# A two-layer network behind a light convolution, one core: TensorE reads the two halves of its moving tile in turns, and ScalarE and GpSimd take over work of VectorE and ScalarE

## The chip, the cores and the metric

The kernel runs on one core of a Trainium2 chip. The metric is the device time in microseconds (us) of one execution. The kernel before took 2235.05 us, the median of three runs (2235.0 to 2235.06).

The core has four engines that compute and run side by side, each taking its own instructions strictly in their order: TensorE (PE in the profile; its weight loads are listed apart as PEld), VectorE (DVE), ScalarE (ACT) and GpSimd (POOL). SyncE (SP) issues the DMAs. TensorE writes into PSUM, an on-chip memory of eight banks of 512 fp32 values per partition; VectorE and ScalarE read it from there. Everything else lies in SBUF.

## The reference

```python
# x: (8, 4096, 192), weight: (8 heads, 7 taps), w_in: (192, 2048), w_out: (2048, 192), all fp32
w = softmax(weight, axis=-1)
out[b, s, h, :] = sum over k of w[h, k] * x_padded[b, s + k, h, :]    # 7 taps, causal, 24 channels a head
x = out.reshape(32768, 192)
h = x @ w_in
g = np.where(h >= 1, h, np.where(h <= -1, 0.0, (h + 1) ** 2 / 4))
return g @ w_out
```

## The kernel before, in words

The 32768 tokens are cut into 64 tiles of 512 (`s`, 0 to 63), and the 2048 hidden features into 8 pairs of 128-feature blocks (`j`, 0 to 7). One step `q = 8 s + j` makes the hidden features of one pair for one tile; there are 512 steps. Two tiles, 16 steps, make a round (`i = q % 16`), and the convolution of a later pair of tiles is spread over the steps of a round.

TensorE does two things in a step. `mm1(q)` (L411) is the first product: 9 pairs of matmuls, each pair being two matmuls of 64 rows that run side by side in the two halves of the array, with 512 moving columns; they fill `h`, two PSUM banks, of which there are two sets (`ps_h`, bufs=2). `mm2(q - 2)` (L451) is the second product of the step two before: 10 such pairs, which add into four PSUM banks `accm0`, `accm1`, `accr0`, `accr1`; these exist once, so the second product of the next tile has to wait until ScalarE has copied them out. From the second round on all operands are split into a high part (fp32r) and a low remainder, `hi`/`lo` of x, `gh`/`gl` of g and two parts of each weight. The first 16 steps (`q < NF32`) work otherwise, in plain fp32 with the roles of the operands swapped in the second product, and are not touched.

Between the two products stands the activation, which the other engines do in each step, in this order of their queues:

- ScalarE: `act_hi(q-1)` (L480, g to gh), `act_square(q)` (L468).
- VectorE: `act_clip(q)` (L462, clips h to -1..1 out of PSUM), `act_lo(q-1)` (L486, gl = g - gh, both inputs in SBUF), `act_max(q)` (L473, max of h and the square). Only `act_max` sets the banks of h free.

Further work hangs on certain steps of a round. In steps 1 and 9 ScalarE copies the four `acc` banks of the tile that was just finished (`evac`, L497 and L498) behind its square, and GpSimd adds them (`sum`, L500). In steps 2 and 10 come a copy and an add of the rest (L510, L511), and in steps 2, 3, 10, 11 VectorE transposes the sums (L523) for the stores. The convolution has three units in a round, called `b`, `a` and `r`, with 7 taps each: a transpose on VectorE (`T`, L147), the product of tap 0 on ScalarE (L226), six products on ScalarE (`product`, L219), six adds on GpSimd (L230), and then the split: a copy on ScalarE (L248, L262) and a subtraction on GpSimd (L252) or VectorE (L263). Which tap falls into which step is a table:

```python
    PLAN_B = {0: (0, 1), 2: (2, 3), 3: (4, 5), 4: (6,), 5: "split"}
    PLAN_A = {4: ("T", 0), 5: (1, 2), 6: (3, 4), 7: (5, 6), 8: "split"}
    PLAN_R = {7: ("T",), 8: (0, 1, 2), 10: (3, 4), 11: (5, 6), 13: "split"}
```

In a step these taps stand behind `act_max` and `act_square`; unit `b` is transposed at the end of step 15. The order of each engine's queue is the order in which the program is written. The functions `both_square` (relu of h/2 + 1/2, then its square, both on ScalarE) and `most` (min with 1, max with h, on VectorE) exist already and are used in the first steps (L742, L744, L749).

Of the kernel before, what the change touches and what calls it, by code (L numbers as in the profile page):

```python
# [13 lines left out]
AF = mybir.ActivationFunctionType  # L14
ALU = mybir.AluOpType
# [3 lines left out]
P = 128  # L19
TB = 512  # L20
# [10 lines left out]
def lightconv_then_ffn(ctx: ExitStack, tc: tile.TileContext, x, weight, w_in, w_out, out):  # L31
# [24 lines left out]
    nc = tc.nc  # L56
    B, S, D = x.shape
# [7 lines left out]
    NPAIR = NF // 2  # L65
    DR = D - P
    NG = TB // SQ + 1
    TOP, BOT = slice(0, DR), slice(DR, P)
    HALVES = (TOP, BOT)
# [14 lines left out]
    def load_raw(t0s, chans, engs=None, n=TB):  # L84


        raw = xin.tile([P, NG, SQ], F32, name="raw")
        first = [t0 % S == 0 for t0 in t0s]
        for i0 in (0, 2):
            if first[i0]:  # L90
                nc.gpsimd.memset(raw[i0 * SQ:(i0 + 2) * SQ, 0, :], 0.0)
        for i in range(4):
            lo = 1 if first[i] else 0
            src = xf[t0s[i] - SQ + lo * SQ:t0s[i] + n, chans[i]:chans[i] + SQ]
            (engs[i] if engs else nc.sync).dma_start(
                out=raw[i * SQ:(i + 1) * SQ, lo:n // SQ + 1, :],
                in_=src.rearrange("(j a) b -> a j b", a=SQ),
            )
        return raw
# [10 lines left out]
    def load_unit(c, u, engs=None):  # L110
# [5 lines left out]
            return load_raw([ta, ta, tb, tb], [P, P + SQ, P, P + SQ], engs)  # L116
        return load_raw([ta if u == "a" else tb] * 4, [0, SQ, 2 * SQ, 3 * SQ], engs)

    xop = [dict() for _ in range(NSB)]

    pending = []
# [10 lines left out]
    NF32 = 2 * NPAIR  # L132
    SH = NG * SQ - TB - (K - 1)

    class Conv:
# [80 lines left out]

        def product(self, k):
            p = xw.tile([P, TB], F32, name="p", bufs=3)
            nc.scalar.mul(p, self.xT[:, SH + k:SH + k + TB], wk[:, self.wsel, k:k + 1])  # L219
            return p  # L220

# [77 lines left out]
    wk = const.tile([P, 2, K], F32, name="wk")  # L299
    warm = const.tile([P, 1], F32, name="warm")  # L300
    whose = const.tile([P, 2 * P + 72], F32, name="whose")[:, 0:2 * P]
    ident = const.tile([P, P], F32, name="ident")
# [87 lines left out]
    NQ = NSB * NPAIR  # L390
    hs, g32, gs, ghs, gls, accs = {}, {}, {}, {}, {}, {}

    def mm1(q):

        s, j = divmod(q, NPAIR)

        if q == 0:
            h = hs[q] = [ps_o.tile([P, TB], F32, name=n) for n in ("accr1", "accm0")]
        else:
            h = hs[q] = ps_h.tile([P, 2, TB], F32, name="h")  # L400
            h = [h[:, e, :] for e in range(2)]

        if s == 0:
            mms = [(WI[j], us, [xop[s][u] for u in us]) for us in ("ns", "sn", "rr")]
        else:
            mms = [(W[j][:, part], u + u, [xop[s][u, x]] * 2) for u in "nsr"
                   for part, x in ((0, "hi"), (1, "hi"), (0, "lo"))]
        for n, (w, us, x) in enumerate(mms):
            for e in range(2):
                c0 = COL[us[e]][e]  # L410
                nc.tensor.matmul(h[e], w[HALVES[e], c0:c0 + P], x[e][e],  # L411
                                 start=(n == 0), stop=(n == len(mms) - 1))

    def new_accs(s):
        accs[s] = {(a, i): ps_o.tile([P, TB], F32, name=f"acc{a}{i}")
                   for a in "mr" for i in range(2)}
# [16 lines left out]
    def mm2(q):  # L433

        s, j = divmod(q, NPAIR)
        gh, gl = ghs.pop(q), gls.pop(q)
        w, wr, k = W[j + LAG], WR[j + LAG], n_in[j + LAG]
        if j == 0:
            new_accs(s)
        m0, m1, r0, r1, r = ("m", 0, gh), ("m", 1, gh), ("m", 0, gl), ("r", 0, gh), ("r", 0, gl)  # L440
        mms = [(e, m) for ms in ((m0, m1), (r0,), (r1,), (r,)) for e in range(2) for m in ms]
        if q == NQ - 1:
            mms = [(0, m) for m in (r1, m0, m1, r, r0)] + [(1, m) for m in (r1, r, m0, m1, r0)]
        first = {a: min(n for n, (e, m) in enumerate(mms) if m[0] == a) for a in "mr"}
        last = {a: max(n for n, (e, m) in enumerate(mms) if m[0] == a) for a in "mr"}
        for n, (e, (a, part, g)) in enumerate(mms):
            c0 = k + e * P
            for i in range(2):
                st = (w[HALVES[i], part, c0:c0 + P] if a == "m"
                      else wr[HALVES[i], e].rearrange("p a d -> p (a d)"))  # L450
                nc.tensor.matmul(accs[s][a, i], st, g[HALVES[i], e, :],  # L451
                                 start=(j == 0 and n == first[a]),
                                 stop=(j == NPAIR - 1 and n == last[a]))


    def tiles(q):
        return [slice(0, 1), slice(1, 2)] if q == NQ - 1 else [slice(0, 2)]

    def act_clip(q):
        g = gs[q] = act.tile([P, 2, TB], F32, name="g", bufs=3)  # L460
        for e in tiles(q):
            nc.vector.tensor_scalar(out=g[:, e, :], in0=hs[q][:, e, :], scalar1=-1.0, scalar2=1.0,  # L462
                                    op0=ALU.max, op1=ALU.min)

    def act_square(q):
        g = gs[q]
        for e in tiles(q):
            nc.scalar.activation(g[:, e, :], g[:, e, :], AF.Square, bias=0.5, scale=0.5)  # L468

    def act_max(q):  # L470
        h, g = hs.pop(q), gs[q]
        for e in tiles(q):
            nc.vector.tensor_tensor(out=g[:, e, :], in0=h[:, e, :], in1=g[:, e, :], op=ALU.max)  # L473
        if q < NF32:
            g32[q] = gs.pop(q)
# [14 lines left out]
    def evac(s):  # L490

        acc = accs.pop(s)
        n = slice(0, 2 * D if s * NPAIR < NF32 else TB)
        for a in "mr":
            t = [ob.tile([P, TB], F32, name="t", bufs=4) for _ in range(2)]
            y = ob.tile([P, TB], F32, name="sum")
            nc.scalar.copy(t[0][:, n], acc[a, 0][:, n])  # L497
            nc.scalar.copy(t[1][:, n], acc[a, 1][:, n])  # L498
            if s > 0:
                nc.gpsimd.tensor_add(y[:, n], t[0][:, n], t[1][:, n])  # L500
            else:
                late.append((y[:, n], t[0][:, n], t[1][:, n]))
            sums[s, a] = y
# [32 lines left out]
    def evac_last(s):  # L536


        acc = accs.pop(s)
        half, rest = slice(0, TB // 2), slice(TB // 2, TB)  # L540
        part = {}
        for a in "rm":
            u, v = [ob.tile([P, TB], F32, name="t", bufs=4) for _ in range(2)]
            for n in (half, rest):
                nc.scalar.copy(u[:, n], acc[a, 0][:, n])
                nc.vector.tensor_tensor(out=v[:, n], in0=acc[a, 1][:, n], in1=u[:, n], op=ALU.add)
            part[a] = v
        ps = [ps_h.tile([P, 2, TB], F32, name="h")[:, 0] for _ in range(2)]
        ps += [ps_o.tile([P, TB], F32, name=f"accr{i}") for i in range(2)]
        y = [ob.tile([P, TB], F32, name="sum") for _ in range(2)]  # L550
        for b in range(TB // P):
            nc.tensor.matmul(ps[b][:, P:D], part["r"][:, b * P:(b + 1) * P], ident[:, 0:DR],  # L552
                             start=True, stop=True)
        for i in range(2):
            for b in (2 * i, 2 * i + 1):
                nc.tensor.transpose(ps[b][:, 0:P], part["m"][:, b * P:(b + 1) * P], plain)
            for b, copy in ((2 * i, nc.scalar.copy), (2 * i + 1, nc.vector.tensor_copy)):
                copy(y[i][:, b % 2 * D:(b % 2 + 1) * D], ps[b][:, 0:D])
                if i == 1:
                    (nc.sync if b % 2 else nc.scalar).dma_start(  # L560
                        out=out[s * TB + b * P:s * TB + (b + 1) * P],
                        in_=y[i][:, b % 2 * D:(b % 2 + 1) * D])
            if i == 0:
                nc.sync.dma_start(
                    out=out[s * TB:s * TB + 2 * P].rearrange("(b p) d -> p b d", p=P),
                    in_=y[i][:, 0:2 * D].rearrange("p (b d) -> p b d", b=2))
# [180 lines left out]
    def most(h, g):  # L747

        nc.vector.scalar_tensor_tensor(out=g, in0=g, scalar=1.0, in1=h, op0=ALU.min, op1=ALU.max)  # L749
# [75 lines left out]
    for q in range(NQ + DELAY):  # L825
        s, j = divmod(q, NPAIR)
        c, i = divmod(q, 2 * NPAIR)
# [11 lines left out]
        if q < NQ:  # L839
            mm1(q)  # L840
# [7 lines left out]
        else:  # L848
# [6 lines left out]
            if q < NQ:  # L855
                let_go()
                act_clip(q)
                act_square(q)
            if done % NPAIR == NPAIR - 1 and done >= NPAIR:
                (evac if done < NQ - 1 else evac_last)(done // NPAIR)  # L860
# [10 lines left out]
            m, r = (DELAY, DELAY + 1) if s > 1 else (NPAIR - 2, NPAIR - 1)  # L871
# [7 lines left out]
        if q == NQ - 4:  # L879
            plain = ob.tile([P, TB // SQ, SQ], F32, name="osb").rearrange("p j b -> p (j b)")[:, 0:P]  # L880
# [27 lines left out]
```

## Time and profile before

| | |
|---|---|
| median of the runs | 2235.05 us (2235.0 to 2235.06) |
| profiled execution, first to last instruction | 2233.2 us |
| PE busy | 2227.3 us (100%) |
| PEld busy | 1850.7 us (83%) |
| DVE busy | 2093.3 us (94%) |
| ACT busy | 1693.7 us (76%) |
| POOL busy | 1173.8 us (53%) |
| DMA | 110.84 MB, mean 50 GB/s |

The page is of one execution under the profiler. Its span leaves out what lies before the first and behind the last instruction; against the median of the timed runs that is 1.85 us, so that a change of the span can be read as a change of the time. Busy time counts only that an engine holds an instruction: matmuls overlap, and a PE busy all the time need not be one at its highest rate.

### The profile page before, as it was taken

Reading aid. Unit: us, or ns where it says so; the run is one execution under the profiler, and the core shown is the slowest. Engines: PE = TensorE matmul, PEld = TensorE weight load, DVE = VectorE, ACT = ScalarE, POOL = GpSimd, SP = SyncE. Lnnn points to the kernel's source line nnn. Section 1 sums busy time; section 2 is a strip of 40 time slices with the busy share of each in tenths; the row PEclk is TensorE's granted clock in tenths of the full one; section 3 lists DMA queues with packets and bytes.
Section 4 is the critical chain, followed back from the end, with each engine's and each line's share of the span. In section 5 each row is a group of like instructions: output and inputs, shape, how many; then the busy total and the mean of one; then the engine's idle time right before and its main releaser. Section 6 shows DMA issues by size and latency. Waiting matters only on the chain.

```text
span 2233.2 us, 48204 instructions
## 1 busy us (share of the span) xinstructions
PE 2227.3 (100%) x19646; PEld 1850.7 (83%) x19646; DVE 2093.3 (94%) x1883; ACT 1693.7 (76%) x2153; POOL 1173.8 (53%) x868
## 2 busy tenths in 40 slices
PE   9999999999999999999999999999999999999999
PEld 6988888888888888888888888888888888888887
DVE  8899999999999999999999999999999999999998
ACT  7677877778777787777877777877778777787775
POOL 1456644556545565455664456644556545565451
PEclk9999999999999999999999999999999999999999
DMA  6222222221222212222122222222221222212211
GB/s 160 49 52 48 42 47 47 52 53 39 52 49 46 54 34 52 49 49 51 40 47 48 49 51 50 41 49 46 50 54 39 52 49 46 54 34 52 49 34 25
DMA packets 442125, 110.84 MB, mean 50 GB/s; under 512 B 410288, under 2 KB 417840, under 8 KB 441904
## 3 DMA queue, kind: packets, MB, share of 16 engines
q1 hardware_dynamic: 441744, 107.66, 24.5%
q8 instruction: 155, 2.54, 0.5%
q14 instruction: 66, 0.54, 0.1%
q10 hardware_dynamic: 160, 0.10, 0.0%
HBM read 32.84 MB, written 25.17 MB: 26 GB/s over the span
## 4 chain that ended last, share of the span: by engine, by line
PE 99%; ACT 0%; DMA 0%; DVE 0%; issue 0%; DVEq 0%; ACTq 0%
PE h L411 47%; PE accm L451 30%; PE accr L451 20%; PE accr L429 1%; PE accm L429 1%; PE accr L190 0%; PE accr L411 0%; DMA osb<-in_weight_dram 0%; PE accm L181 0%; PE h L552 0%; ACT xT L168 0%; ACT xT L165 0%; ACT xT L167 0%; PE accm L411 0%; PE h L155 0%
## 5 line engine op out<-in xcount | busy, mean ns | idle before, releaser
L230 POOL TENSOR_TENSOR y<-y,p 128x512 f32<-128x512 f32 x546 | 798.2, 1462 | 733.3 <-DVE g L473 560.7
L411 PE MATMUL h<-hi,w 64*128 64x512 f32 x4032 | 764.7, 387 | 0.0
L486 DVE TENSOR_TENSOR gl<-g,gh 128x1024 fp32r<-128x1024 f32 (+1 forms) x497 | 730.4, 1470 | 29.3 <-ACT gh L480 24.2
L468 ACT ACTIVATE g<-g 128x1024 f32<-128x1024 f32 (+1 forms) x505 | 535.5, 1061 | 234.8 <-DVE g L462 228.5
L480 ACT CAST gh<-g 128x1024 fp32r<-128x1024 f32 (+1 forms) x497 | 522.8, 1052 | 226.8 <-DVE g L473 185.2
L462 DVE TENSOR_SCALAR g<-h 128x1024 f32<-128x1024 f32 (+1 forms) x505 | 609.1, 1206 | 85.5 <-PE h L411 84.4
L451 PE MATMUL accm<-gh,w 64*128 64x512 f32 x3968 | 639.6, 387 | 0.0
L473 DVE TENSOR_TENSOR g<-h,g 128x1024 f32<-128x1024 f32 (+1 forms) x505 | 613.3, 1215 | 11.8 <-ACT g L468 4.5
L411 PEld LDWEIGHTS h<-hi,w 64*128 64x128 f32 x4032 | 561.3, 185 | 75.4
L411 PE MATMUL h<-lo,w 64*128 64x512 f32 x2016 | 613.0, 387 | 0.0
L451 PEld LDWEIGHTS accm<-gh,w 64*128 64x128 f32 x3968 | 463.6, 184 | 75.6
L451 PE MATMUL accr<-gh,wr 64*128 64x512 f32 x1984 | 414.8, 387 | 0.0
L451 PE MATMUL accr<-gl,wr 64*128 64x512 f32 x1984 | 414.8, 386 | 0.0
L451 PE MATMUL accm<-gl,w 64*128 64x512 f32 x1984 | 414.7, 387 | 0.0
L411 PEld LDWEIGHTS h<-lo,w 64*128 64x128 f32 x2016 | 371.3, 184 | 38.1 <-DMA lo<-lo 0.2
L219 ACT ACTIVATE p<-xT,wk 128x512 f32<-128x512 f32 x562 | 374.9, 709 | 0.0
L451 PEld LDWEIGHTS accm<-gl,w 64*128 64x128 f32 x1984 | 276.4, 184 | 37.9
L451 PEld LDWEIGHTS accr<-gh,wr 64*128 64x128 f32 x1984 | 276.3, 184 | 37.8
L451 PEld LDWEIGHTS accr<-gl,wr 64*128 64x128 f32 x1984 | 276.2, 184 | 37.9
L411 PE MATMUL h<-rhi,w 64*128 64x512 f32 x992 | 304.1, 386 | 0.0
L411 PE MATMUL h<-rh,w 64*128 64x512 f32 x992 | 304.1, 386 | 0.0
L500 POOL TENSOR_TENSOR sum<-t 128x512 f32<-128x512 f32 (+1 forms) x124 | 157.4, 1291 | 101.8 <-ACT t L498 101.8
(143 smaller groups left out, 1945.4 us busy)
## 6 DMA issues: line engine op xcount, KB each, us to landing
out_dram<-osb SPq DMA_DIRECT2D x366, 64.0 KB, 1.9
raw<-in_x_dram SPq DMA_DIRECT2D x334, 68.0 KB, 2.4
hi<-hi SPq DMA_DIRECT2D x126, 128.0 KB, 2.3
lo<-lo SPq DMA_DIRECT2D x126, 128.0 KB, 2.3
rhi<-rh SPq DMA_DIRECT2D x62, 128.0 KB, 2.2
rlo<-rl SPq DMA_DIRECT2D x62, 128.0 KB, 2.3
words<-in_moe_w_in_dram SPq DMA_DIRECT2D x16, 192.0 KB, 3.6
words<-in_moe_w_out_dram SPq DMA_DIRECT2D x8, 384.0 KB, 4.8
```

What stands on the lines that cost most here:

```text
L219: nc.scalar.mul(p, self.xT[:, SH + k:SH + k + TB], wk[:, self.wsel, k:k + 1])
L230: nc.gpsimd.tensor_add(y, y, self.product(k))
L411: nc.tensor.matmul(h[e], w[HALVES[e], c0:c0 + P], x[e][e], start=(n == 0), stop=(n == len(mms) - 1))
L429: nc.tensor.matmul(accs[s][a, i][:, c0:c0 + D], g[half, e, b * P:(b + 1) * P], w[half, e, :], start=(j == 0 and e == 0 and b % 2 == 0), st ...
L451: nc.tensor.matmul(accs[s][a, i], st, g[HALVES[i], e, :], start=(j == 0 and n == first[a]), stop=(j == NPAIR - 1 and n == last[a]))
L462: nc.vector.tensor_scalar(out=g[:, e, :], in0=hs[q][:, e, :], scalar1=-1.0, scalar2=1.0, op0=ALU.max, op1=ALU.min)
L468: nc.scalar.activation(g[:, e, :], g[:, e, :], AF.Square, bias=0.5, scale=0.5)
L473: nc.vector.tensor_tensor(out=g[:, e, :], in0=h[:, e, :], in1=g[:, e, :], op=ALU.max)
L480: nc.scalar.copy(gh[:, e, :], gs[q][:, e, :])
L486: eng.tensor_sub(gl[:, e, :], g[:, e, :], gh[:, e, :])
L500: nc.gpsimd.tensor_add(y[:, n], t[0][:, n], t[1][:, n])
```

## The change

The moving operand of a matmul was read column by column, 0 to 511. Now `turns` makes TensorE read column 0, 256, 1, 257 and so on: the halves of the tile in turns. The result is written to consecutive columns of PSUM, so the tokens come out in another order. In the first product this holds from tile 2 on (`in_turns`), in the second always. Passing two products, the tokens are permuted twice, and `evac` undoes it: its ScalarE copies read PSUM in order and write SBUF in steps of 128 elements. The last tile is put in order by the products that transpose it, which read every fourth column.

In 8 of the 16 steps of a round (`BY_ACT`) the clip of VectorE is left out; ScalarE makes a relu out of PSUM and a square of it instead, two instructions where it had one, and VectorE's maximum becomes the three-input `most`. Six of the 21 tap products of a round (`BY_POOL`) move from ScalarE to GpSimd. This begins with step 16 and the third pair of tiles.

```diff
+    BY_POOL = (('b', 4), ('b', 5), ('a', 5), ('a', 6), ('r', 5), ('r', 6))
...
         def product(self, k):
             p = xw.tile([P, TB], F32, name="p", bufs=3)
+            if self.c > 1 and (self.u, k) in BY_POOL:
+                nc.gpsimd.tensor_scalar(out=p, in0=self.xT[:, SH + k:SH + k + TB],
+                                        scalar1=wk[:, self.wsel, k:k + 1], scalar2=None,
+                                        op0=ALU.mult)
+                return p
             nc.scalar.mul(p, self.xT[:, SH + k:SH + k + TB], wk[:, self.wsel, k:k + 1])
...
+    def turns(t):
+        return t.rearrange("p (o c) -> p c o", o=2)
+    def both(t):
+        return t.rearrange("p (c o) -> p c o", o=2)
+    def in_turns(s):
+        return s * NPAIR >= NF32
...
-                nc.tensor.matmul(h[e], w[HALVES[e], c0:c0 + P], x[e][e],
+                to, of = (both(h[e]), turns(x[e][e])) if in_turns(s) else (h[e], x[e][e])
+                nc.tensor.matmul(to, w[HALVES[e], c0:c0 + P], of,
...
-                nc.tensor.matmul(accs[s][a, i], st, g[HALVES[i], e, :],
+                nc.tensor.matmul(both(accs[s][a, i]), st, turns(g[HALVES[i], e, :]),
...
+    BY_ACT = (3, 4, 7, 11, 12, 13, 14, 15)
+    def by_act(q):
+        return q % (2 * NPAIR) in BY_ACT and NF32 <= q < NQ - 2
     def act_clip(q):
         g = gs[q] = act.tile([P, 2, TB], F32, name="g", bufs=3)
+        if by_act(q):
+            nc.scalar.activation(g, hs[q], AF.Relu, bias=0.5, scale=0.5)
+            return
...
     def act_square(q):
         g = gs[q]
+        if by_act(q):
+            nc.scalar.activation(g, g, AF.Square)
+            return
...
-        for e in tiles(q):
+        if by_act(q):
+            most(h, g)
+        for e in () if by_act(q) else tiles(q):
             nc.vector.tensor_tensor(out=g[:, e, :], in0=h[:, e, :], in1=g[:, e, :], op=ALU.max)
...
-            nc.scalar.copy(t[0][:, n], acc[a, 0][:, n])
-            nc.scalar.copy(t[1][:, n], acc[a, 1][:, n])
+            for i in range(2):
+                to, of = t[i][:, n], acc[a, i][:, n]
+                if in_turns(s):
+                    to = to.rearrange("p (b o a) -> p a b o", b=2, o=2)
+                    of = of.rearrange("p (a b o) -> p a b o", b=2, o=2)
+                nc.scalar.copy(to, of)
...
-            nc.tensor.matmul(ps[b][:, P:D], part["r"][:, b * P:(b + 1) * P], ident[:, 0:DR],
+            nc.tensor.matmul(ps[b][:, P:D], part["r"][:, b::TB // P], ident[:, 0:DR],
...
-                nc.tensor.transpose(ps[b][:, 0:P], part["m"][:, b * P:(b + 1) * P], plain)
+                nc.tensor.transpose(ps[b][:, 0:P], part["m"][:, b::TB // P], plain)
```

Three places show what this does to the queues. In the listings a row is one instruction (xN: N alike in a row): line, operation, out<-in and size. The lines of the changed kernel are its own: L485 is the relu, L494 its square, L497 the square of the other steps, L511 gh, L254 the copy hi, L232 and L225 tap products, L533 the copies out of the accumulators; on GpSimd L221 is a product, L236 an add, L258 the subtraction of the split; on VectorE L488 is the clip, L517 gl, L504 and L784 the maximum in its two forms, L148 the transpose.

ScalarE before, from the end of step 7 into step 9 of a round:

```order
L219 ACTIVATE p<-xT,wk 128x512 x2
L480 CAST gh<-g 128x1024
L468 ACTIVATE g<-g 128x1024
L248 CAST hi_15422<-y 128x512
L226 ACTIVATE y<-xT,wk 128x512
L219 ACTIVATE p<-xT,wk 128x512 x2
L480 CAST gh<-g 128x1024
L468 ACTIVATE g<-g 128x1024
L497 COPY t<-accm_15045 128x512
```

ScalarE in the changed kernel, from step 7 into step 9:

```order
L485 ACTIVATE g<-h 128x1024
L494 ACTIVATE g<-g 128x1024
L511 CAST gh<-g 128x1024
L497 ACTIVATE g<-g 128x1024
L254 CAST hi_15422<-y 128x512
L232 ACTIVATE y<-xT,wk 128x512
L225 ACTIVATE p<-xT,wk 128x512 x2
L511 CAST gh<-g 128x1024
L497 ACTIVATE g<-g 128x1024
L533 COPY t<-accm_15045 128x128x4
```

The two products of step 7 are gone from ScalarE and a relu stands ahead of its square; the four tap and split instructions of step 8 still stand ahead of gh of step 8, of the square of step 9 and of the copies out of the accumulators.

GpSimd before, from the adds that end unit b (steps 3 and 4) to the first adds of unit r in step 8:

```order
L230 TENSOR_TENSOR y<-y,p 128x512 x3
L252 TENSOR_TENSOR lo_11564<-y,hi_11563 128x512
L230 TENSOR_TENSOR y<-y,p 128x512 x6
L252 TENSOR_TENSOR lo_11736<-y,hi_11735 128x512
L230 TENSOR_TENSOR y<-y,p 128x512 x2
```

GpSimd in the changed kernel, the same stretch:

```order
L236 TENSOR_TENSOR y<-y,p 128x512 x2
L258 TENSOR_TENSOR lo_15251<-y,hi_15250 128x512
L236 TENSOR_TENSOR y<-y,p 128x512 x4
L221 TENSOR_SCALAR p<-xT,wk 128x512
L236 TENSOR_TENSOR y<-y,p 128x512
L221 TENSOR_SCALAR p<-xT,wk 128x512
L236 TENSOR_TENSOR y<-y,p 128x512
L258 TENSOR_TENSOR lo_15423<-y,hi_15422 128x512
```

Between the split of b and the split of a GpSimd now has eight instructions where it had six; the copy `hi` of unit a on ScalarE waits for the last of them.

VectorE before, steps 15 and 0:

```order
L462 TENSOR_SCALAR g<-h 128x1024
L486 TENSOR_TENSOR gl<-g,gh 128x1024
L473 TENSOR_TENSOR g<-h,g 128x1024
L147 STREAM_TRANSPOSE xT<-raw 128x544
L462 TENSOR_SCALAR g<-h 128x1024
L486 TENSOR_TENSOR gl<-g,gh 128x1024
```

VectorE in the changed kernel, steps 15 and 0:

```order
L517 TENSOR_TENSOR gl<-g,gh 128x1024
L784 SCALAR_TENSOR_TENSOR g<-g,h 128x1024
L148 STREAM_TRANSPOSE xT<-raw 128x544
L488 TENSOR_SCALAR g<-h 128x1024
L517 TENSOR_TENSOR gl<-g,gh 128x1024
L504 TENSOR_TENSOR g<-h,g 128x1024
```

The clip of step 15 is gone; that of step 0 stands, as before, behind the maximum of step 15 and the transpose of unit b.

## The prediction

> **What bounds the kernel now.** I read the page first (busy time, clock, the chain that ended last), then who TensorE waits for, then its timeline.
>
> ```profile
> PE 2227.3 (100%) x19646; PEld 1850.7 (83%) x19646; DVE 2093.3 (94%) x1883; ACT 1693.7 (76%) x2153; POOL 1173.8 (53%) x868
> PEclk9999999999999999999999999999999999999999
> PE 99%; ACT 0%; DMA 0%; DVE 0%; issue 0%; DVEq 0%; ACTq 0%
> PE accm L597 <- POOL osb L601: 1.2, 1, 1.2
> ```
>
> TensorE is the whole chain, at full clock, and its longest wait in the run is 1.2 us at the start. VectorE is close behind (94%). So time can come only out of the pace of the matmuls, and any engine that falls behind shows at once.
>
> ```profile
> 999.85 0.84 PE L411 MATMUL h<-hi,w 64*128 64x512 f32 x4
> ...
> 1001.89 1.29 PE L451 MATMUL accm<-gh,w 64*128 64x512 f32 x8
> ...
> 1004.16 0.84 PE L411 MATMUL h<-hi,w 64*128 64x512 f32 x4
> 38.25 1.91 PE L411 MATMUL h<-hi,gl 64*128 64x512 f32 x8
> ...
> 40.83 0.85 PE L429 MATMUL accm<-wf,g 64*128 64x192 f32 x8
> 41.48 0.85 PE L429 MATMUL accr<-wf,g 64*128 64x192 f32 x8
> ```
>
> A step is 1004.16 - 999.85 = 4.31 us for 19 pairs, 226.7 ns a pair; a round of 16 is 68.9 us. The early plain-fp32 matmuls pass each column twice: 6 pairs of 512 columns from 38.25 to 40.83 are 430 ns each, 4 pairs of 192 from 40.83 to 41.48 are 162.5 ns. The difference, 267.5 ns over 320 columns, is 0.418 ns a column and pass, with 2 ns fixed: 512 columns once would be 216 ns. The split matmuls lose 10.7 ns a pair against that. Weight loads aren't the reason, as the 192-column pairs load as many weights every 162.5 ns.
>
> **The change: reading in turns.** No row has a matmul that reads in steps. It touches 62 x 8 x 9 first-product pairs and 62 x 8 x 10 second-product pairs, 9424. Ends: all the loss goes (-10.7 ns x 9424 = -101 us, 2134), or nothing does; a loss beyond is a rival below. I take 216 ns, the nearest row at a slower read. A step is then 4.10 us and a round 65.6. The last tile's 8 products that read every fourth column, and one more order of PSUM columns, are under 1 us even doubled. No DMA is added or moved.
>
> **Relu on ScalarE, in 8 steps of a round.** VectorE loses 246 clips; ScalarE gains 246 relus of 1.01 us and loses 180 products. By sums both fit (DVE about 1800, ACT about 1815 us). But the clip was the one link that TensorE alone triggered. Without it each step hangs on the one before: gh(q-1), relu(q), square(q), maximum(q) on VectorE, gh(q), all in ScalarE's order.
>
> ```profile
> L742 ACT ACTIVATE g<-h 128x1024 f32<-128x1024 f32 x7 | 7.1, 1014 | 2.4 <-PE h L411 2.4
> L749 DVE SCALAR_TENSOR_TENSOR g<-g,h 128x1024 f32<-128x1024 f32 x7 | 8.5, 1214 | 0.0
> 14.98 0.60 ACT L761 ACTIVATE g<-accr 128x512 f32<-128x512 f32 x1 [0.64 <-PE accm L411]
> 15.61 0.63 ACT L764 ACTIVATE g<-g 128x512 f32<-128x512 f32 x1
> 1108.10 1.06 ACT L468 ACTIVATE g<-g 128x1024 f32<-128x1024 f32 x1 [0.61 <-DVE g L462]
> 1109.19 1.23 DVE L473 TENSOR_TENSOR g<-h,g 128x1024 f32<-128x1024 f32 x1
> 1110.51 1.05 ACT L480 CAST gh<-g 128x1024 fp32r<-128x1024 f32 x1 [1.35 <-DVE g L473]
> 1089.70 1.06 ACT L468 ACTIVATE g<-g 128x1024 f32<-128x1024 f32 x1 [0.79 <-DVE g L462]
> 1090.67 0.60 ACT L248 CAST hi<-y 128x512 fp32r<-128x512 f32 x1
> 1091.18 0.72 ACT L226 ACTIVATE y<-xT,wk 128x512 f32<-128x512 f32 x1
> 1091.81 1.32 ACT L219 ACTIVATE p<-xT,wk 128x512 f32<-128x512 f32 x2
> 1093.04 1.04 ACT L480 CAST gh<-g 128x1024 fp32r<-128x1024 f32 x1
> 1094.01 1.06 ACT L468 ACTIVATE g<-g 128x1024 f32<-128x1024 f32 x1
> 1094.98 0.57 ACT L497 COPY t<-accm 128x512 f32<-128x512 f32 x1
> 1095.44 0.59 ACT L498 COPY t<-accm 128x512 f32<-128x512 f32 x1
> 1096.42 1.09 PEld L451 LDWEIGHTS accm<-gh,w 64*128 64x128 f32 x8
> 1086.56 1.21 DVE L473 TENSOR_TENSOR g<-h,g 128x1024 f32<-128x1024 f32 x1
> 1087.70 0.73 DVE L147 STREAM_TRANSPOSE xT<-raw 128x544 f32<-128x544 f32 x1
> 1088.45 1.23 DVE L462 TENSOR_SCALAR g<-h 128x1024 f32<-128x1024 f32 x1
> 1089.59 2.05 DVE L486 TENSOR_TENSOR gl<-g,gh 128x1024 fp32r<-128x1024 f32 x1
> 1079.38 1.30 POOL L252 TENSOR_TENSOR lo<-y,hi 128x512 fp32r<-128x512 f32 x1 [3.75 <-ACT hi L248]
> 1080.65 9.91 POOL L230 TENSOR_TENSOR y<-y,p 128x512 f32<-128x512 f32 x6
> ```
>
> These rows carry the sum. On ScalarE the next instruction starts before the last has ended: gh to square is 0.97 us (1093.04 to 1094.01), products 0.61 each, copies out of `acc` 0.46; where one needs the other's result, 0.03 passes (14.98 + 0.60 to 15.61), 0.03 to VectorE (1109.16 to 1109.19), 0.09 back (1110.42 to 1110.51). So gh to relu 0.97, relu 1.01 + 0.03, square 1.06 + 0.03, maximum 1.21 + 0.09: **4.40 us a step**, longer than TensorE's 4.10 and even than 4.31. Steps 11 to 15 are five such steps in a row.
>
> Behind step 9 stands what can't give: ScalarE ended the second copy of accm at 1095.44 + 0.59 = 1096.03, and TensorE loaded weights for that bank at 1096.42, 0.39 us later. And at 1090.67 the copy hi of unit a started 0.11 us after GpSimd's six adds ended (1080.65 + 9.91 = 1090.56).
>
> **Once round, from relu(11):** I follow the three queues, each instruction starting when its engine and its inputs are free.
> - To the end of maximum(15): 4 x 4.40 + 1.04 + 1.09 + 1.21 = 20.9.
> - VectorE transposes b (0.66), clips step 0 (1.25), ScalarE squares (1.09), maximum (1.14), clip of step 1 (1.25), square (0.96), copies (0.49 + 0.59): 7.4. They stand in line behind maximum(15), so the clip now comes late.
> - GpSimd's two sums (1.30 each) hold up gl(1), whose like was stretched from 1.21 to 2.05 us at 1089.59; gl(1), maximum(2), gh(2): 5.9.
> - Steps 3 and 4: 4.40; relu, square, maximum 3.3, transpose a 0.77, tap 0 0.61, gh 0.95, square(5) 0.97, hi of b 0.66: 11.7.
> - GpSimd: split and six adds 11.2 as in the rows, two products at 0.85, one more wait for gl 0.9: 13.8.
> - ScalarE in step 8 and 9: hi 0.54, y 0.61, two products 1.22, gh and square 1.92, two copies 1.1: 5.4.
> - Back to relu(11): two copies, gh, square, two products, the rest's copy 4.6, wait for maximum(10) 0.75, gh 0.95: 6.3.
>
> Sum **71.4 us** a round, whatever TensorE's pace is below that: 2.5 more than now. The matmuls' gain of 3.3 us a round turns into waits of second products for `acc`, some 5.8 us a round, most in steps 10 and 2.
>
> **Unknown prices in it.** A GpSimd product has no row.
>
> ```profile
> L614 POOL MEMSET whose<- 128x256 f32 x1 | 0.3, 312 | 0.0
> L531 POOL MEMSET ident<- 128x128 f32 x1 | 0.2, 205 | 0.0
> L500 POOL TENSOR_TENSOR sum<-t 128x512 f32<-128x512 f32 x122 | 155.4, 1296 | 98.9 <-ACT t L498 98.9
> L497 ACT COPY t<-accm 128x512 f32<-128x512 f32 x61 | 34.6, 566 | 0.0
> L497 ACT COPY t<-accm 128x384 f32<-128x384 f32 x2 | 0.9, 458 | 0.0
> ```
>
> Ends: a write without a read, 0.31 + 256 x 0.84 ns = 0.53 us, where the wait for gl in unit a's stretch also falls away and the round is 69.9; and two inputs, 1.30, 72.5. I take 0.85, between, for one input. By the Trainium skill (GPSIMD Engine Reference, Elementwise, side-by-side cycle accounting) a tight loop over 512 elements takes 769 ns; the round would be an estimated 71.2, and no run here shows it yet. The copies out of `acc` now write in steps of 512 bytes. Ends: nothing, or their 0.43 us of data time (566 - 458 ns for 128 elements, times 4) over again, 2.3 us a round more; less than nothing is excluded, as the same values are moved. I take 0.05, nearest to the plain rows, 0.1 a round.
>
> **Sum.** The profiled span is 2233.2 us, 1.85 under the median; I add to the median. The loop closes 30 times (from round 1 to 31): 30 x 2.5 = 75. The first steps of round 1 and the last of round 31 still run at 4.10, 2 us off. 2235 + 75 - 2 = **2308 us**. With the ends above: 2263 to 2341, at the far end of the copies 2407.
>
> **Rivals.**
> - *The engines keep up, and TensorE's gain counts.* The banks of h are double and gh, gl triple; if the lag of steps 11 to 15 is worked off before step 1, TensorE stays the bound: 2235 - 101 = 2134, and with a wait of 0.2 to 1.6 us a round 2140 to 2185. For it: both engines fit by sums, 88% at most. Against it: the 4.40 us and the 0.39 us. It decides where a round of the three queues is under 68.9 us. 23%.
> - *The two cancel*, round at 68.9: 2235. 5%.
> - *Reading in turns slows the matmuls.* Each read then jumps 1024 bytes. From 235 ns a pair (a round of 71.4) TensorE is again the bound; at two column times, 428 ns, 9424 x 201 ns = 1.9 ms more, 4130. For it speaks only that no row has such a read. 6%. The Trainium skill (SBUF — State Buffer, Specifications) says that SBUF lines are 16 bytes and need two hits each for full bandwidth, so this pattern would pay; no run here shows it.
> - *The reading changes nothing* (226.7 ns): the same 2308, as TensorE isn't in the loop; its chance is within mine.
>
> **Chances.** Slower by the loop 66%, engines keep up 23%, cancel 5%, slower matmuls 6%. So faster by over 0.2% 0.23, within 0.2% (about what a measurement here can tell) 0.05, slower 0.72. The forecast's own range is 2263 to 2350. The range that holds 8 in 10 has to take in cases of both signs: 2140 to 2350.
>
> **What would show it.** Right: pairs at 216 ns where TensorE runs, TensorE waiting for ScalarE's copies (`accm` for `t`) in steps 10 and 2 by some us, ScalarE's hi of unit a waiting for GpSimd's add, gh waiting for the maximum in steps 11 to 15 at 4.4 us a step, rounds of 71 us. Wrong: a TensorE without waits in the middle of the run; pairs above 227 ns; GpSimd products far from 0.85 us; copies of `acc` near 1 us.

## The result, and the profile after

The changed kernel takes 2431.6 us (2431.2 to 2432.0) against 2235.1 before, a ratio of 1.088 (95% interval 1.086 to 1.089): 196.5 us slower, where 73 were forecast. Slower was right, but by far too little. First the page of the kernel after, its busy times (us, share, count) and the shares of the chain that ended last:

```profile
PE 2246.6 (92%) x19646; PEld 1901.8 (78%) x19646; DVE 1860.8 (77%) x1637; ACT 1907.0 (78%) x2219; POOL 1522.0 (63%) x1048
ACT 33%; PE 24%; POOL 19%; DVE 14%; issue 7%; SPq 2%; DMA 1%; POOLq 0%; DVEq 0%; ACTq 0%
```

The span and the mean granted clock, which was 1.000 before:

```profile
core 0: 2429.7 us, clock 0.964
```

What TensorE waits for (us in total, times, longest):

```profile
PE accm L468 <- ACT t L533: 153.4, 76, 4.6
PE accm L468 <- DVE gl L517: 12.8, 29, 0.6
```

And five rows of its timeline (start, us, line, operands, count, wait ahead of it):

```profile
1001.74 1.13 PE L468 MATMUL accm<-gh,w 64*128 64x512 f32 x7 [0.41 <-ACT t L533]
...
1008.42 0.80 PE L428 MATMUL h<-hi,w 64*128 64x512 f32 x4
...
1012.53 0.80 PE L428 MATMUL h<-hi,w 64*128 64x512 f32 x4
...
1040.61 2.98 PE L468 MATMUL accm<-gh,w 64*128 64x512 f32 x8 [4.56 <-ACT t L533]
...
1077.12 1.13 PE L468 MATMUL accm<-gh,w 64*128 64x512 f32 x7 [0.41 <-ACT t L533]
```

TensorE's share of the chain fell from 99% to 24%; ScalarE, GpSimd and VectorE hold 66% together. Where TensorE runs, it does what was hoped: a step takes 1012.53 - 1008.42 = 4.11 us, 216 ns a pair. But once a round, in step 10, its second product waits 4.56 us for ScalarE's copies out of `acc`, and a round is 1077.12 - 1001.74 = 75.4 us instead of 68.9. And the eight matmuls behind that wait take 2.98 us instead of 1.2: TensorE's granted clock (its share of full speed) has fallen, which in the kernel before stayed whole. Now the groups of the two operations that had no row before (count, busy us, mean ns):

```profile
L221 POOL TENSOR_SCALAR p<-xT,wk 128x512 f32<-128x512 f32 x180 | 368.0, 2045 | 0.0
L533 ACT COPY t<-accr 128x512 f32<-128x512 f32 x122 | 123.1, 1113 | 0.0
L533 ACT COPY t<-accm 128x512 f32<-128x512 f32 x122 | 118.6, 1075 | 0.0
```

And the timelines of GpSimd in the stretch of unit a (from the split of unit b to the last add of unit a), of VectorE during GpSimd's second product there, and of ScalarE behind it:

```profile
1019.95 1.38 POOL L258 TENSOR_TENSOR lo<-y,hi 128x512 fp32r<-128x512 f32 x1 [0.85 <-ACT hi L254]
1021.29 7.15 POOL L236 TENSOR_TENSOR y<-y,p 128x512 f32<-128x512 f32 x4
1028.42 1.56 POOL L221 TENSOR_SCALAR p<-xT,wk 128x512 f32<-128x512 f32 x1
1030.07 1.28 POOL L236 TENSOR_TENSOR y<-y,p 128x512 f32<-128x512 f32 x1
1031.33 2.54 POOL L221 TENSOR_SCALAR p<-xT,wk 128x512 f32<-128x512 f32 x1
1033.95 1.28 POOL L236 TENSOR_TENSOR y<-y,p 128x512 f32<-128x512 f32 x1
...
1030.94 1.49 DVE L517 TENSOR_TENSOR gl<-g,gh 128x1024 fp32r<-128x1024 f32 x1
...
1035.26 0.62 ACT L254 CAST hi<-y 128x512 fp32r<-128x512 f32 x1 [3.14 <-POOL y L236]
```

A product of one input takes GpSimd 1.56 us while VectorE's `gl` (two inputs out of SBUF) is not running, and 2.54 us beside it (once 1.56, once 2.54 in the rows above). The 180 products are of these two kinds alone, in halves: 91 took 1.55 to 1.60 us, 89 took 2.50 to 2.60, and every one of the long ones lay beside `gl`. An add with two inputs takes 1.28. So ScalarE's copy hi waits 3.14 us for GpSimd, and behind hi stand gh, square and the copies out of `acc`, which now take 1.1 us each instead of 0.57 and 0.60.

### The profile page after: what moved, and what is told of

The parts are those of the page before. It is cut to its first block, busy times and chain, and to the rows that moved or that the text cites. A ratio compares the mean times of both kernels' runs of the same rounds, so it can differ in the third digit from the quotient of the medians.

```text
span 2429.7 us, 47443 instructions
## 1 busy us (share of the span) xinstructions
PE 2246.6 (92%) x19646; PEld 1901.8 (78%) x19646; DVE 1860.8 (77%) x1637; ACT 1907.0 (78%) x2219; POOL 1522.0 (63%) x1048
## 4 chain that ended last, share of the span: by engine, by line
ACT 33%; PE 24%; POOL 19%; DVE 14%; issue 7%; SPq 2%; DMA 1%; POOLq 0%; DVEq 0%; ACTq 0%
POOL y L236 12%; PE h L428 11%; ACT t L533 8%; ACT gh L511 7%; DVE g L784 7%; PE accm L468 6%; POOL p L221 5%; PE accr L468 5%; ACT g L497 5%; ACT g L494 4%; ACT g L485 4%; DVE g L488 3%; ACT p L225 2%; ACT y L232 2%; DVE xT L148 2%
## 5 line engine op out<-in xcount | busy, mean ns | idle before, releaser
L236 POOL TENSOR_TENSOR y<-y,p 128x512 f32<-128x512 f32 x546 | 755.1, 1383 | 585.9 <-DVE g L504 466.7
L517 DVE TENSOR_TENSOR gl<-g,gh 128x1024 fp32r<-128x1024 f32 (+1 forms) x497 | 770.3, 1550 | 420.2 <-ACT gh L511 417.7
L511 ACT CAST gh<-g 128x1024 fp32r<-128x1024 f32 (+1 forms) x497 | 519.4, 1045 | 290.5 <-DVE g L784 264.7
L428 PE MATMUL h<-hi,w 64*128 64x512 f32 x4032 | 708.1, 379 | 0.0
L428 PE MATMUL h<-lo,w 64*128 64x512 f32 x2016 | 544.8, 377 | 0.0
L784 DVE SCALAR_TENSOR_TENSOR g<-g,h 128x1024 f32<-128x1024 f32 x253 | 308.2, 1218 | 124.0 <-ACT g L494 119.7
L221 POOL TENSOR_SCALAR p<-xT,wk 128x512 f32<-128x512 f32 x180 | 368.0, 2045 | 0.0
L428 PEld LDWEIGHTS h<-lo,w 64*128 64x128 f32 x2016 | 332.8, 187 | 27.4 <-DMA lo<-lo 0.4
L497 ACT ACTIVATE g<-g 128x1024 f32<-128x1024 f32 x259 | 273.1, 1055 | 58.1 <-DVE g L488 55.3
L504 DVE TENSOR_TENSOR g<-h,g 128x1024 f32<-128x1024 f32 x259 | 313.2, 1210 | 4.3 <-ACT g L497 4.2
L488 DVE TENSOR_SCALAR g<-h 128x1024 f32<-128x1024 f32 x259 | 310.1, 1198 | 7.5 <-PE h L428 7.2
```

The lines of the kernel that those rows point to most:

```text
L221: nc.gpsimd.tensor_scalar(out=p, in0=self.xT[:, SH + k:SH + k + TB], scalar1=wk[:, self.wsel, k:k + 1], scalar2=None, op0=ALU.mult)
L236: nc.gpsimd.tensor_add(y, y, self.product(k))
L428: nc.tensor.matmul(to, w[HALVES[e], c0:c0 + P], of, start=(n == 0), stop=(n == len(mms) - 1))
L511: nc.scalar.copy(gh[:, e, :], gs[q][:, e, :])
L517: eng.tensor_sub(gl[:, e, :], g[:, e, :], gh[:, e, :])
```

## The experiments

Twelve kernels. Where not said otherwise, each edit is made to the changed kernel.

**1. Reading in turns alone, with straight copies.** Of the change only the matmuls' reading is left.

```diff
-    BY_POOL = (('b', 4), ('b', 5), ('a', 5), ('a', 6), ('r', 5), ('r', 6))
+    BY_POOL = ()
...
-    BY_ACT = (3, 4, 7, 11, 12, 13, 14, 15)
+    BY_ACT = ()
...
-                if in_turns(s):
-                    to = to.rearrange("p (b o a) -> p a b o", b=2, o=2)
-                    of = of.rearrange("p (a b o) -> p a b o", b=2, o=2)
```

> Only the reading in turns is left: relu and the six products are back on VectorE and ScalarE, and the copies out of acc are straight, so that the output's tokens stand in the wrong order. Theory (three queues form a loop, and what is long in it sets the round): matmuls at 216 ns a pair, copies back near 0.57 us; VectorE and ScalarE keep up but for waits of 1 to 2 us a round, so 2185 us (2150 to 2210). Rival (the turned reading itself costs, by the halved clock after waits): no wait over 2 us, clock still under 0.98, time over 2235. If TensorE alone were the bound: 2134.

2170.3 us, ratio 0.971 (0.970 to 0.973). The reading gains 64.8 us of the possible 101. The only waits of TensorE inside the loop, at most 0.3 us each:

```profile
PE accm L468 <- ACT t L530: 9.1, 28, 0.3
```

The rest of the missing 36 us lies in waits too short for this view. By the starts of its matmuls, TensorE loses 1.2 us a round, in steps 6, 9 and 10, and 30 x 1.2 = 36.

**2. Reading in turns with its reordering copies**, `BY_ACT` and `BY_POOL` empty as in the first.

> Reading in turns with its reordering copies out of acc, without relu on ScalarE and without products on GpSimd. Theory: the copies of 1.1 us instead of 0.57 put 2.1 us on ScalarE in steps 1 and 9 each, TensorE waits for them in steps 2 and 10: a round of 71.0 us, 2298 us (2260 to 2330), so this change is a loss by itself. Rival (GpSimd's products alone made the loss): about 2185, as without the reordering.

2262.7 us, ratio 1.013 (1.011 to 1.014): slower than before. So the edit to the matmuls, with what it needs to put the tokens back into order, is a loss of 28 us by itself, and the reordering copies cost 92 us. TensorE waits in both places where `acc` is copied:

```profile
PE accm L468 <- ACT t L533: 47.9, 90, 0.8
PE accr L468 <- ACT t L533: 15.9, 61, 0.3
```

**3. The engines' share alone.** Matmuls, copies and the last tile read straight as before; relu on ScalarE and the six products on GpSimd stay. The diff leaves out the lines of the copies, which are the last three of the first diff, and those of the last tile.

```diff
-                to, of = (both(h[e]), turns(x[e][e])) if in_turns(s) else (h[e], x[e][e])
+                to, of = (both(h[e]), turns(x[e][e])) if False else (h[e], x[e][e])
...
-                nc.tensor.matmul(both(accs[s][a, i]), st, turns(g[HALVES[i], e, :]),
+                nc.tensor.matmul(accs[s][a, i], st, g[HALVES[i], e, :],
...
```

> Relu on ScalarE and the six products on GpSimd, with matmuls and copies read straight as in the kernel before. Theory: the loop of the three queues is longer than TensorE's 68.9 us a round by itself: products of 1.56 us, or 2.54 us beside gl, give rounds of 72.8 us, 2354 us (2320 to 2400), though TensorE's pace is the old one. Rival (the reordering copies alone made the loss): 2235 or a little less.

2412.2 us (2406.9 to 2416.0), ratio 1.079 (1.078 to 1.081): well above the rival's 2235, and above my own 2354. What is missing in the theory shows in the chain that ended last (start, us, what):

```profile
1031.44 0.47 ACT t L530
...
1031.95 3.40 PE accm L468 x12
...
1039.51 1.36 PE accm L468 x12
...
1067.61 2.05 PE h L428 x18
1069.69 1.23 DVE g L488
```

Behind the wait the chain runs through TensorE for 38 us. Its first 12 matmuls of `accm` take 3.40 us where 1.36 is usual. The mean granted clock is 0.960.

**4. The changed kernel with straight copies**, the last three lines of the first diff alone.

> The changed kernel with straight copies out of acc (the output's tokens stand in the wrong order). Theory: the same loop as with the engines' share alone, as TensorE isn't in it: 72.8 us a round, 2354 us (2320 to 2400), the same within 1% as the run with straight reading, so the faster matmuls bring nothing. Rival (copies alone): under 2200. Rival (products alone): 2430, unchanged.

2360.1 us, ratio 1.056 (1.055 to 1.058). The time is the theory's, but it is 52 us less than with straight reading, so TensorE's pace does count (run 7 shows by what way). The copies, back at 574 and 598 ns, are worth 71.5 us here.

**5 and 6. One engine's share alone, in the kernel before.** Both have the diff of the third; 5 has `BY_POOL = ()` besides, 6 `BY_ACT = ()`.

> The kernel before with relu and square on ScalarE in the eight steps as the only change: straight reading, no product on GpSimd. Theory (serial loop of 4.40 us a step in steps 11 to 15, the clip of step 0 late behind it, waits of some tenths in steps 2 and 10 too short for the clock to fall): 69.7 us a round, 2259 us (2240 to 2275). Rival (VectorE and ScalarE keep up, only the products hurt): 2235.

> The kernel before with the six products on GpSimd as the only change. Theory: GpSimd's chain of unit a (four adds, products of 1.56 and 2.54 us, two adds) makes ScalarE's copy hi late, behind it square, copies out of acc and TensorE: 72.5 us a round by the queues, with the halved clock after a wait of over 3 us up to 75.1, so 2345 to 2425 us, I take 2400. Rival (relu on ScalarE is what hurts): under 2260.

Relu alone: 2252.8 us, ratio 1.008 (1.006 to 1.009), 17 us slower, as the theory had it; no wait of TensorE in the loop is long enough to be listed. The products alone: 2409.1 us (2401.1 to 2415.4), ratio 1.078 (1.075 to 1.081), the same as both together. Among the waits of the products alone, ScalarE waits for GpSimd once a round, and TensorE for ScalarE:

```profile
ACT hi L254 <- POOL y L236: 121.0, 32, 4.1
PE accm L468 <- ACT t L530: 89.1, 30, 4.0
```

**7 and 8. The clock.** The waiting time is partly filled with work: twelve more pairs ahead of the first product of step 10, whose sums are thrown away, as the matmul behind them begins a new sum (`start`). 7 is the engines' share alone (2412.2 us), 8 the changed kernel.

```diff
+        again = 12 if q % 16 == 10 and q > NF32 else 0
-        for n, (w, us, x) in enumerate(mms):
+        for m, (w, us, x) in enumerate(mms[:1] * again + mms):
+            n = max(m - again, 0)
...
-                                 start=(n == 0), stop=(n == len(mms) - 1))
+                                 start=(n == 0), stop=(m < again or n == len(mms) - 1))
```

> The engines' share alone (2412 us), with 12 more pairs of matmuls at the head of the first product of step 10 in each round from the second on (its first pair over again, whose sums the next one clears), 2.7 us of work put into a wait of 2.9 us. Clock theory (the wait lets the clock fall to a half for 3.4 or 6.8 us, and TensorE catches up too slowly): no halved clock, a round of 72.8 instead of 75, 2354 us (2335 to 2375), faster though it does more. Rival (the halved clock is hidden, the queues alone set the round): 2412, unchanged; if the added matmuls lie on the path, 2412 + 31 x 2.7 = 2496.

> The changed kernel (2431.6 us) with the same 12 pairs at the head of the first product of step 10, 2.6 us of a wait of 4.6. Theory (its chain of waits goes through ScalarE's copies of 1.1 us, not through the slow stretch): the halved clock goes, and the time falls little, to 2400 to 2432. Rival (the clock sets this round too, as 22 windows of 3.413 us are 75.1): 2360 or less. On the path: 2510.

7 took 2368.1 us, ratio to before 1.060 (1.058 to 1.061): 44 us less than without the added matmuls, though TensorE does 31 x 2.7 us more. So in run 3 the fallen clock cost 44 us: TensorE, slowed down behind the wait, did not catch up. The mean granted clock is 1.000, and TensorE's waits inside the loop are down from 87.3 us in total to 10.4:

```profile
PE accm L470 <- ACT t L532: 10.4, 29, 0.6
```

8 took 2428.7 us, ratio 1.087 (1.085 to 1.088), 3 us less than the changed kernel. The added matmuls fill only a part of the wait: waits of up to 2.0 us are left, and with them a mean clock of 0.982; the slow time fell from 178 to 91 us. But four rounds in a row, from 1642.9 us on, had no slow stretch, and they can be held against the others of the same run. The first copy of `accm` starts at 1567.51, 1642.87 and 1718.24 us: the round with a slow stretch takes 75.36 us, the one without 75.37 (stretch, its length, busy us of each engine, granted clock, DMA):

```profile
1567.50:1642.90 75.40, 71.75 (x632) 60.67 (x632) 57.83 (x49) 59.64 (x70) 49.24 (x33) 0.98 0.23 44
1642.90:1718.20 75.30, 70.72 (x632) 60.29 (x632) 57.75 (x49) 59.55 (x69) 49.14 (x33) 1.00 0.23 43
```

The changed kernel's own rounds, with slow stretches of mostly 6.83 us, take 75.4 us as well. So here the fallen clock is hidden: the queues set the round, as the theory had it.

**9. The order put back by the stores.** Reading in turns alone, straight copies, and a DMA that writes each row of 128 bytes to its token.

```diff
-            engs[i % len(engs)].dma_start(out=dst.rearrange("(j a) b -> a j b", a=SQ),
+            engs[i % len(engs)].dma_start(out=dst.rearrange("(o j a) b -> a o j b", o=4, a=SQ // 4),
                                           in_=osb[i * SQ:(i + 1) * SQ])
```

> Reading in turns alone with straight copies out of acc, where the DMAs of the stores bring the tokens back into order (128 bytes each, as before, to other rows). Theory: the order costs nothing there, 2170 us as without it (2165 to 2180). Rival: the four-part pattern makes the stores later or their issue longer, waits of GpSimd or VectorE for the sums' buffers, over 2200.

2170.0 us, ratio 0.971 (0.970 to 0.972), the same as the first: the order costs nothing there.

**10. A version that beats both.** The ninth with three tables changed:

```diff
-    BY_ACT = ()
+    BY_ACT = (3,)
...
-    PLAN_A = {4: ("T", 0), 5: (1, 2), 6: (3, 4), 7: (5, 6), 8: "split"}
-    PLAN_R = {7: ("T",), 8: (0, 1, 2), 10: (3, 4), 11: (5, 6), 13: "split"}
+    PLAN_A = {3: ("T",), 4: (0,), 5: (1, 2), 6: (3, 4), 7: (5, 6), 8: "split"}
+    PLAN_R = {8: ("T",), 9: (0,), 10: (1, 2), 11: (3, 4), 12: (5, 6), 13: "split"}
```

> As the run before with relu on ScalarE in step 3 alone, the transpose of unit a in step 3 instead of 4, the transpose of unit r in step 8 instead of 7 and its taps 0 to 6 in steps 9 to 12. Theory (queues leave 1.2 us of waits a round in steps 6, 9 and 10, which the earlier end of unit a and a lighter step 8 take away): TensorE alone bounds, 65.6 to 66.0 us a round, 2134 to 2150 us. Rival: the waits only move, 2170.

2134.8 us (2134.5 to 2134.9), ratio 0.955 (0.954 to 0.957): the whole 100 us that reading in turns can bring. TensorE is busy throughout by the page, and no wait of its inner loop is long enough to be listed:

```profile
PE 2126.7 (100%) x19646; PEld 2005.7 (94%) x19646; DVE 1981.5 (93%) x1852; ACT 1722.5 (81%) x2184; POOL 1245.9 (58%) x868
```

Which of the three tables did it was not taken apart.

**11. The changed kernel without the products on GpSimd**, `BY_POOL = ()`.

> The changed kernel without the products on GpSimd. Theory (GpSimd's price is the largest of the terms that I set too low): relu on ScalarE and copies of 1.1 us are left, 72.2 us a round, 2335 us (2300 to 2350), so the products are worth some 95 us. Rival (copies and relu alone set the 75 us): 2400 or more.

2316.1 us, ratio 1.036 (1.035 to 1.038). The products are worth 115.5 us of the 196.5, more than the copies (71.5, run 4). Against run 2, which differs by relu alone, it is 53 us more: beside reordering copies and faster matmuls, relu costs three times as much as in run 5.

**12. Ways to read.** A measurement, with the copies of `accm` reading in steps of 16 bytes and writing straight; `BY_ACT` and `BY_POOL` are empty as in the first.

```diff
+    WAYS = (2, 4, 8, 16, 32, 64, 128, 256, 1)
...
-                to, of = (both(h[e]), turns(x[e][e])) if in_turns(s) else (h[e], x[e][e])
+                to, of = h[e], x[e][e]
+                if in_turns(s):
+                    of = of.rearrange("p (o c) -> p c o", o=WAYS[n])
+                    to = to.rearrange("p (c o) -> p c o", o=WAYS[n])
...
-                if in_turns(s):
-                    to = to.rearrange("p (b o a) -> p a b o", b=2, o=2)
-                    of = of.rearrange("p (a b o) -> p a b o", b=2, o=2)
+                if in_turns(s) and a == "m":
+                    to = to.rearrange("p (b o a) -> p b o a", b=2, o=2)
+                    of = of.rearrange("p (a b o) -> p b o a", b=2, o=2)
```

> A measurement within one kernel: the nine pairs of the first product read their 512 columns in turns out of 2, 4, 8, 16, 32, 64, 128 and 256 pieces and, the ninth, straight; the first two copies of each tile read acc in steps of 16 bytes and write straight, the last two are straight (what it computes is another order of columns). Theory A (any read that isn't column after column is free of the loss): 216 ns for the first eight, 226.7 ns for the ninth. Theory B (pieces near each other fall into the same part of the memory): 216 ns for 2 to some number of pieces, 226.7 ns or more from there on. Copies: 0.57 us if only the scattered write costs, 1.1 if any reordering does.

Theory A was wrong. What B foretold came in outline (two pieces are fast, many are not), but a time twice as long was in neither, and B's reason is not shown by it. The timeline of one step, where the rows follow the order of the pairs (2 and 4 pieces, 8, 16 and 32, 64, 128, 256, straight), and then a second product that reads its two halves in turns:

```profile
1003.55 0.83 PE L433 MATMUL h<-hi,w 64*128 64x512 f32 x4
1004.04 0.85 PE L433 MATMUL h<-lo,w 64*128 64x512 f32 x2
1004.53 1.24 PE L433 MATMUL h<-hi,w 64*128 64x512 f32 x4
1005.41 0.79 PE L433 MATMUL h<-lo,w 64*128 64x512 f32 x2
1005.84 0.64 PE L433 MATMUL h<-rh,w 64*128 64x512 f32 x1
...
1006.30 0.63 PE L433 MATMUL h<-rh,w 64*128 64x512 f32 x1
...
1006.75 0.42 PE L433 MATMUL h<-rl,w 64*128 64x512 f32 x1
...
1007.01 1.19 PE L473 MATMUL accm<-gh,w 64*128 64x512 f32 x8
1007.88 0.76 PE L473 MATMUL accm<-gl,w 64*128 64x512 f32 x4
```

Two pieces in turns keep 216 ns (1007.01 to 1007.88 for four pairs). By the starts of the single pairs, one with 8 pieces or more takes 434 to 482 ns (by the rows, 8: 1004.53 - 1004.04 = 0.49; 16 and 32: 0.88 together; 64: 0.43), twice as long. 4 pieces (278 ns) and the straight pair (260) stand at the edges of the slow stretch, and how much of that is their own isn't told apart.

The copies out of `acc`, `accr` straight and `accm` read in steps:

```profile
L538 ACT COPY t<-accr 128x512 f32<-128x512 f32 x122 | 66.3, 605 | 0.0
L538 ACT COPY t<-accm 128x512 f32<-128x512 f32 x122 | 64.8, 584 | 0.0
```

Reading PSUM in steps costs nothing (584 ns against 605 straight; in run 1, straight, 579 and 606), so it was the scattered write that doubled them.

## Why the prediction had the loop right and its prices wrong

**Reading in turns, 216 ns a pair, a step of 4.10 us: right** (4.11 us). Run 10 makes the whole of it into time, 2134.8 us against the 2134 that the sum of the pairs gave.

**The loop of ScalarE, VectorE and GpSimd, whatever TensorE's pace is: right for the changed kernel, wrong where the clock falls and TensorE is slower (below).** ScalarE in the changed kernel, with the relus of steps 3, 11 and 15 and the first copies of steps 1 and 9:

```profile
999.74 1.95 ACT L533 COPY t<-accm 128x512 f32<-128x512 f32 x2
...
1008.17 1.02 ACT L485 ACTIVATE g<-h 128x1024 f32<-128x1024 f32 x1
...
1039.53 1.94 ACT L533 COPY t<-accm 128x512 f32<-128x512 f32 x2
...
1047.93 1.02 ACT L485 ACTIVATE g<-h 128x1024 f32<-128x1024 f32 x1
...
1065.50 1.02 ACT L485 ACTIVATE g<-h 128x1024 f32<-128x1024 f32 x1
...
1075.11 1.96 ACT L533 COPY t<-accm 128x512 f32<-128x512 f32 x2
```

Four steps in 1065.50 - 1047.93 = 17.57 us are 4.39 each, 4.40 by the sum. The waits came in steps 10 and 2, and hi of unit a waits for GpSimd, as told. Run 5 gives the part of relu by itself: 17 us, 24 by the theory.

**The step that failed is that of the unknown prices.** The round was to be 71.4 us and is 75.4. With the rows above and those of the split and of hi behind the result, each stretch of the sum can be held against the trace:

| stretch of the round | by the sum | in the trace |
|---|---|---|
| first copies of step 1 to relu(3) | 5.9 | 6.5 (1001.69 to 1008.17) |
| to the split of unit b | 11.7 | 11.8 (to 1019.95) |
| GpSimd, to hi of unit a | 13.8 | 15.3 (to 1035.26) |
| ScalarE in steps 8 and 9, to the end of the first copies | 5.4 | 6.2 (to 1041.47) |
| to relu(11) | 6.3 | 6.5 (to 1047.93) |
| to the end of the first copies of step 1 | 28.3 | 29.1 (to 1077.07) |
| a round | 71.4 | 75.4 |

- *GpSimd's product, taken at 0.85 us, costs 1.56.* I had bounded it from above by the add of two inputs, 1.30, on the thought that one input cannot cost more than two. It can. The 2.54 us of the other kind are 1.56 and another 1 us beside `gl`, for which the sum had 0.9 as a wait. Two products with that wait are 4.1 us instead of 2.6: 1.5 us a round.
- *The copies out of `acc`, taken at 0.05 us more, cost 0.51 more.* They stand in four of the six stretches, which are longer by 0.6, 0.8, 0.2 and 0.8: 2.4 us a round.

With 0.1 in steps 3 and 4 these are the 4.0 us that the sum lacks, and 30 x 4.0 = 120 of the 124 us that the forecast lacks. Runs 4 and 11 take the two away one at a time. Without the scattered writes it is 71.5 us less, for 30 x 2.4 = 72. Without the products it is 115.5 us less, as a round is 71.6 us: 3.8 less, of which 3.4 lie between the split of unit b and hi of unit a (11.9 us in run 11, 1046.85 to 1058.77). The clock has no part in that, though its mean is 0.984 there and 0.964 in the changed kernel: in run 11 the round is 71.6 us before the first slow stretch, at 706.8 us, and after it.

A second fault lies in the range. With both prices at their far ends the sum gave 2407 (a round of 72.5 + 2.3 - 0.1 = 74.7 us), yet the range stopped at 2350: two unknowns on the same chain belong together at their far ends. Even 2407 was short of 2431.6, as the far end of the products, 1.30, was no bound, and that of the copies, 0.43 more, was a little low.

**The clock wasn't in the prediction at all.** It costs the changed kernel nothing, but only because TensorE has time to spare there. Here is the wait of step 10 in the changed kernel (stretch, its length, busy us of each engine, granted clock, DMA):

```profile
1036.10:1038.40 2.30, 0.00 (x0) 0.00 (x0) 0.00 (x0) 2.30 (x4) 2.30 (x2) 1.00 0.51 119
1038.60:1040.60 2.00, 0.00 (x0) 0.00 (x0) 1.91 (x1) 2.00 (x4) 1.20 (x1) 0.50 0.45 102
1040.60:1045.10 4.50, 4.37 (x19) 3.12 (x21) 3.48 (x4) 4.50 (x6) 2.55 (x2) 0.50 0.00 0
1045.40:1049.50 4.10, 4.10 (x40) 3.57 (x38) 3.51 (x4) 4.02 (x6) 3.58 (x3) 1.00 0.18 33
```

TensorE's matmuls end at 1036.05, the clock is halved from 1038.5 to 1045.2, and some 4.6 us of matmuls run at half speed. "Whatever TensorE's pace" holds only while it can catch up: with straight reading (4.31 us a step against a loop of 4.39) it can't, and the fallen clock costs 44 us (runs 3 and 7). At 4.11 us a step it can: the rounds of run 8 take 75.4 us with a slow stretch and without.

**The rivals.** "The engines keep up" is false for this order of the queues; its 2134 us are reached by another order, without the products, with one relu and with the tokens put back by the stores (run 10). "Reading in turns slows the matmuls" is false for two halves and true from eight pieces on, where the 428 ns that it priced are 434 to 482. By the Trainium skill (SBUF — State Buffer, Specifications) an access that jumps to another 16-byte line each time pays. The doubled time for pieces agrees with that; that two halves in turns pay nothing, though each read jumps 1024 bytes, does not, and neither do 256 pieces, which are every second column, so that two reads in a row fall into one line, and still a pair takes 453 ns. The measurement decides; why two halves are free and eight pieces are not stays open.

## What to carry to other kernels

A faster bottleneck is worth only what the other engines leave of it: before an instruction is moved to an engine with time to spare, follow the queue in which it will stand, and ask what is behind it. Put a reordering where the data is moved in small pieces anyway: in the stores it cost nothing, in the copies out of PSUM it cost more than the matmuls gained. An operation that has no row yet should be measured alone before it is put on a loop; its neighbour in the list is no bound. And where several prices on one chain are unknown, the range has to hold all of them at their far ends together.

## What was not expected of the hardware

Inside the loop the granted clock falls and rises on a grid of 3.41 us. A slow stretch lasts 3.41 or 6.83 us, and the starts of two of them lie whole units apart: 75.1 us, 22 units, 26 times out of 30 in the changed kernel, and 71.7 us, 21 units, 21 times out of 22 in run 11. In these two runs that is only the counting in units, as their rounds, 75.4 and 71.6 us, don't follow the clock. In run 3 the round does lock to the grid: it is 73.2 us at first, grows to 75.1 with the slow stretches and stays there.

It takes less than a full unit without work: in run 11 the clock fell behind waits of 1.32 and 0.42 us, with one matmul between them, where the waits of at most 0.8 us in run 2 left it whole. The timeline of TensorE in run 11, and the stretch that follows (length, busy us of the engines, granted clock, DMA):

```profile
992.48 0.48 PE L468 MATMUL accm<-gh,w 64*128 64x512 f32 x1 [1.32 <-ACT t L533]
993.38 1.96 PE L468 MATMUL accm<-gh,w 64*128 64x512 f32 x7 [0.42 <-ACT t L533]
```

```profile
993.90:996.90 3.00, 3.00 (x18) 2.36 (x16) 2.02 (x3) 3.00 (x5) 2.05 (x2) 0.50 0.00 0
```

What counts is how the wait lies on the grid. In the rounds of run 11 ahead of 706 us TensorE has nearly the same two waits (1.31 and 0.42 us at 491 us and at 634 us), and the clock stayed whole. Counting 216 ns of work from the start of each matmul, the unit just before a fall of the clock holds at most 0.42 of work, in all 160 falls inside the loops of the changed kernel and of runs 3, 4, 6, 8 and 11, and a unit at full clock that no fall follows holds at least 0.39. So by these runs the clock falls behind a unit that is worked for less than about 0.4 of its length.

By the Trainium skill (TensorE: Matmul & The Clock Gate, The HAM clock gate) the gate watches free-running windows of 3413 ns and falls back after an idle one; the unit agrees with the runs, but 1.7 us of standing still was enough here, and the measurement decides.

Straight reading is not the fastest for these fp32r operands: 226.7 ns for 512 columns against 216 when the two halves are read in turns. And on the same 128x512 elements GpSimd's one-input product is slower (1.56 us) than its two-input add (1.28), and takes another 1 us beside VectorE's `gl`.
